# Reordering an attention stage around its gate: a later exponential, four weight quarters, another order for the last chunk

## The chip, the cores and the metric

The kernel runs on one core of a Trainium2 chip. Its time is the device time of one execution in microseconds. TensorE (PE) multiplies matrices, VectorE (DVE), ScalarE (ACT) and GpSimd (POOL) do the rest, and SyncE (SP) issues most of the DMAs; GpSimd issues gathers, scatters and the DMAs that add to what lies in SBUF. Each engine takes its instructions in order. TensorE has a granted clock of 2.4 GHz or half of it.

## The reference

Three layers follow each other. In short:

```
attention (B=2, H=8, S=768, D=48), a linear recurrence per head:
    y[t] = r[t] . (state + (u * k[t]) v[t]^T)
    state = w * state + k[t] v[t]^T
x = y as 1536 tokens of 384
gate: logits = x @ w_gate (8 experts); e = argmax; p = softmax(logits)[e]
    a token has the next free place of its expert; over capacity it is dropped (row 0)
experts: out = p * (relu(x @ w1[e]) @ w2[e]),  w1: 384 x 1024, w2: 1024 x 384
last layer: h = out @ w_in; s = h * softmax(h); layer norm with g_ln; out = ln @ w_out
```

All is float32. The kernel gets near float32 out of single-pass matmuls by splitting an operand in two parts: hi, the rounded value, and lo, the remainder; a product is hi*hi + hi*lo + lo*hi.

## The kernel before, in words

**Attention (to about 85 us).** The 1536 tokens are 12 chunks of 128, six to a batch element. A loop over m = 0..11 does chunk m, and prepares later ones. In the order of the code, a step does: the decay of the state (`decay`, ScalarE), the scores of chunk m+1 (TensorE) and their mask (`mask_scores`, L295, VectorE), the products of chunk m+2 with the decay tables (`prelude`, GpSimd), and then `attend(m)`: `values`, `carry` (the state's part) and `attended` (A*v, L324) add up in PSUM, and ScalarE evicts them (L330). `between` inside `attend` is `ranks(m - 1)`: three small matmuls that count, for each token, how many earlier ones chose the same expert. In steps 1 and 11 they stand behind A*v, in the others ahead of it. `gate2(m - 1)` makes the slot of each token of the chunk before from its rank (L426, L433, L438, L441, L444) and scales the tokens by their gate (L448); `scatter` writes the token numbers to their slots in DRAM, `store` the tokens. `state(m)` updates the state (L362, L366, L371). `tokens(m)` turns chunk m back to tokens and multiplies by w_gate (L382). `gate1(m)` takes the argmax: sum the logits (L391, "lg" in what follows), smallest of the negated ones (L394), candidates (L396), maximum (L402), one-hot row (L404); between the candidates and the maximum the code issues the exponential with its sum on ScalarE (L399). Logits, candidates and rank product share one PSUM bank, and the program guards such a bank against two engines at once.

Beside this the loop loads raw expert weights in halves of 128 x 1536 (`load_half`, four buffers, the table `halves` says in which step) and splits quarters of 128 x 768 (`split_q`): hi on ScalarE (L115), lo on VectorE (L121). With `by_dma`, ScalarE writes -raw, rounded as hi is, into lo (L124), and a DMA issued by GpSimd adds the raw weights to it from DRAM (L119). With `defer=True` the low part waits in `pend` and is issued in the next step, interleaved with `gate2`. Six quarters are split in steps 4 to 9, the sixth by DMA.

**Last chunks.** Expert 0's tokens of chunks 0 to 7 are gathered from DRAM (L93); those of chunks 8 to 11 are placed by matmuls with a one-hot matrix (`place`, L539), with hi and lo of the tokens (`part`, `other`). After chunk 11 the code does gate1, part of gate2, ranks and the placing, then splits the result (L668, L670), and the experts begin. Slots of chunk 11 are scattered, and then expert 1's rows can be gathered: ids (L85) from DRAM, then the rows (L93).

**Experts (to about 221 us).** 32 steps g, four to an expert, each with 18 matmuls of `mm1(g)` (L793) and, two steps later, 18 of `mm2(g)` (L779 to L781). `xe_split` transposes the rows of the next expert (L772) and splits them. Each step also splits a quarter of w1 and of w2 for later steps; of w2, every fourth low part is made by DMA. Buffers: four each of hi and lo, for w1 and w2. Pieces of the last layer's weights are loaded and decoded between.

**Last layer (to the end).** Matmuls, softmax, norm and a scatter of the result per 128 rows.

Of the kernel before, what the change touches and what calls it, by code (L numbers as in the profile page):

```python
# [35 lines left out]
def rwkv_moe_solu_kernel(  # L36
# [95 lines left out]
    def attention(actx):  # L132
# [167 lines left out]
        def attend(m, between):  # L300
# [3 lines left out]
            late = m in (1, NM - 1)  # L304

# [30 lines left out]
            if not late:  # L336
                between()
# [4 lines left out]
            if late:  # L342
                between()
# [44 lines left out]
        def gate1(m):  # L388
            xp = xps[m]
            lg, eqd = banks[m][0:2]  # L390
            V.tensor_reduce(lg, xp[:, :, 2 * D:XW].rearrange("p a e -> p e a"), AX.X, ALU.add, negate=True)  # L391
            yield
            nmx = sm.tile([128, 1], F32, tag="nmx", name=f"nmx{m}")
            V.tensor_reduce(nmx, lg, AX.X, ALU.min)  # L394
            yield
            V.scalar_tensor_tensor(eqd, lg, nmx, desc, ALU.is_le, ALU.mult)  # L396
            ex = sm.tile([128, NE], F32, tag="ex", name=f"ex{m}")
            gs = sm.tile([128, 1], F32, tag="gs", name=f"gs{m}")
            S.activation(ex, lg, AF.Exp, bias=nmx, scale=-1.0, accum_out=gs)  # L399
            yield  # L400
            m2 = sm.tile([128, 1], F32, tag="m2", name=f"m2{m}")
            V.tensor_reduce(m2, eqd, AX.X, ALU.max)  # L402
            yield
            V.tensor_scalar(oh_all[:, m, :], eqd, m2, None, ALU.is_equal)  # L404
            gst[m] = (m2, gs)
            yield
# [11 lines left out]
        def gate2(m):  # L418
            m2, gs = gst.pop(m)
            oh, rk1 = oh_all[:, m, :], rank_all[:, m:m + 1]  # L420
            t1 = sm.tile([128, 1], F32, tag="t1", name=f"t1{m}")
            if m < NM - 2:
                S.activation(t1, m2, AF.Copy, scale=float(-RS), bias=float(NE * RS))
            else:
# [10 lines left out]
            if m == NM - 1:  # L435
                yield
            junk = sm.tile([128, NE], F32, tag="junk", name=f"junk{m}")
            V.scalar_tensor_tensor(junk, rps.pop(m), 1.0, oh, ALU.mult, ALU.mult, accum_out=rk1)  # L438
            yield
            t2 = sm.tile([128, 1], F32, tag="t2", name=f"t2{m}")  # L440
# [5 lines left out]
            yield  # L446
            xg = a2.tile([128, HP, 2 * D], F32, tag="xg", name=f"xg{m}", bufs=LAST + 1)
            S.activation(xg, raw[m][0], AF.Copy, scale=gate)  # L448
            xgs[m] = xg.rearrange("p a d -> p (a d)")
            yield  # L450
# [112 lines left out]
        halves = {2: (1, 0), 4: (2, 0), 5: (1, 1), 6: (2, 1), 7: (1, 2), 8: (1, 3), 10: (2, 2)}  # L563
        pend = []
        for m in range(NM):
            if m != NM - 2:
                decay(m)
            if m == NM - 2:
                pend.pop()()
# [10 lines left out]
            if m == NM - 1:  # L580
                steps = gate2(m - 1)
# [4 lines left out]
                onehots[m - 2] = place(m - 2)  # L586
            elif m:
                together(gate2(m - 1), single(*pend))
                pend.clear()
            if m == NM - LAST + 1:  # L590
                xe0 = load_xe(0, 0, 2, 1 + (NM - LAST) * C, ld.tile([128, 3, DM], F32, tag="kvr", name="xe0"))
            if m + 2 < NM:
                products = prelude2(m + 2)
                next(products)
            if m:
                scatter(m - 1)
            if m < NM - 2:
                state(m)
            tokens(m)
# [6 lines left out]
            if m == NM - 3:  # L606
                decay(m + 1)
# [14 lines left out]
            if 4 <= m < NM - 2:  # L622
                i = m - 4
                pend.append(split_q(1 + (i // 2) % 2, 2 * (i // 4) + i % 2, m == NM - 3, defer=True))
# [22 lines left out]
        next(steps), next(steps)  # L647
        ranks(m)
        onehots[m - 1] = place(m - 1)
        next(steps)  # L650
        onehots[m] = place(m)
        next(steps), next(steps)
        his[m] = part(m)
        together(steps)
        for i in (m - 1, m):
            los[i] = other(i, his[i])
        store(m)
# [22 lines left out]
    def experts_and_solu():  # L680
# [212 lines left out]
        for q in (2, 3):  # L893
            split_q(2, q, False)
        load_piece(0)
        load_piece(1)
        load_half(1, 4)
        for g in range(NQ + 2):
# [15 lines left out]
            if g + 4 < NQ:  # L914
                split_q(1, g + 4, False)
            if 2 <= g < NQ - 2:
                split_q(2, g + 2, g % 4 == 0)
# [6 lines left out]
            if g % 2 and g < NQ:  # L924
                j = (g + 1) // 2
                if 4 < j + 3 < NQ // 2:
# [251 lines left out]
```

## Time and profile before

| | |
|---|---|
| time, median of 3 runs | 344.92 us (343.88 to 345.94) |
| profiled execution | 343.56 us, its span 341.8 us |
| busy | PE 320.6, DVE 244.2, ACT 191.4, POOL 145.7 us |
| granted TensorE clock | 0.982 of 2.4 GHz, mean over the span |
| DMA | 56.61 MB, mean 166 GB/s |

The span counts from the first instruction to the last. Busy times are sums over stages that have different limits, so they have to be read stage by stage. In rows of the trace, times are microseconds from the span's start; L with a number is a line of the kernel; what stands in brackets is how long the engine was idle ahead of the instruction, and which engine's work ended that.

### The profile page before, as it was taken

The numbers are of one execution on the slowest core, as the hardware profiler recorded it, in microseconds if no ns is written. First come the engines' busy times: TensorE is split into PE (matmuls) and PEld (weight loads), VectorE is DVE, ScalarE is ACT, GpSimd is POOL, SyncE is SP. The second block draws the span as 40 slices with busy tenths as digits, with TensorE's granted clock in tenths as the row PEclk, the third lists the DMA queues.
The fourth block names the chain that finished last, engine by engine and source line by source line (L and its number), as shares of the span: only waits on it lengthen the run. The fifth ranks groups of instructions, "written<-read, shape, count | busy, mean of one in ns | idle before, by whom it ended". The sixth has DMA issues, their size and how long they took to land. (4 is left out here: it accounts for less than half of the span.)

```text
span 341.8 us, 7242 instructions
## 1 busy us (share of the span) xinstructions
PE 320.6 (94%) x2656; PEld 297.6 (87%) x2656; DVE 244.2 (71%) x572; ACT 191.4 (56%) x409; POOL 145.7 (43%) x198
## 2 busy tenths in 40 slices
PE   7999977988999999999999999898999999999990
PEld 3788866877999999999999999886999999999990
DVE  8988898976688999998999897365674444444410
ACT  1455646674666787878786956323654444433420
POOL 7977778855314422313241506503333233333321
PEclk9999999998799999999999999999999999999996
DMA  7988899528667989889798933000000000000010
GB/s 226 384 312 284 294 348 324 204 75 202 200 213 271 243 309 306 269 289 296 254 287 279 279 125 52 10 2 1 2 23 23 25 23 23 25 23 25 24 46 23
DMA packets 20394, 56.61 MB, mean 166 GB/s; under 512 B 6594, under 2 KB 8900, under 8 KB 20356
## 3 DMA queue, kind: packets, MB, share of 16 engines
q1 hardware_dynamic: 16772, 47.67, 40.9%
q0 software_dynamic: 3584, 8.46, 10.5%
q8 instruction: 21, 0.34, 0.4%
q14 instruction: 17, 0.14, 0.1%
HBM read 50.96 MB, written 5.16 MB: 164 GB/s over the span
## 5 line engine op out<-in xcount | busy, mean ns | idle before, releaser
L115 ACT ACTIVATE whi<-raw 128x768 fp32r<-128x768 f32 x64 | 52.2, 845 | 7.2 <-PE yps L780 3.5
L121 DVE TENSOR_TENSOR wlo<-raw,whi 128x768 fp32r<-128x768 f32 x56 | 52.1, 962 | 1.1 <-ACT whi L115 0.7
L780 PE MATMUL yps<-hl,whi 128*128 128x224 f32 x192 | 52.8, 275 | 0.0
L779 PE MATMUL yps<-hh,whi 128*128 128x224 f32 x192 | 52.7, 275 | 0.0
L781 PE MATMUL yps<-hh,wlo 128*128 128x224 f32 x192 | 52.4, 273 | 0.0
L1011 POOL TENSOR_SCALAR e<-e,nmu 128x1024 f32<-128x1024 f32 x12 | 13.5, 1122 | 65.8 <-DVE nmu L1010 65.8
L988 DVE TENSOR_REDUCE nm<-h 128x1 f32<-128x1024 f32 (+1 forms) x13 | 14.8, 1140 | 31.2 <-PE h L977 31.2
L780 PEld LDWEIGHTS yps<-hl,whi 128*128 128x128 f32 x192 | 36.9, 192 | 0.0
L781 PEld LDWEIGHTS yps<-hh,wlo 128*128 128x128 f32 x192 | 36.9, 192 | 0.0
L779 PEld LDWEIGHTS yps<-hh,whi 128*128 128x128 f32 x192 | 36.9, 192 | 0.0
L119 POOL DMA_DIRECT2D wlo<-in_w x8 | 7.9, 988 | 64.6 <-ACT wlo L124 55.3
L1045 PE MATMUL o<-w_hi,shi 128*128 128x384 f32 x96 | 33.1, 345 | 0.0
L1046 PE MATMUL o<-w_lo,shi 128*128 128x384 f32 x96 | 32.2, 335 | 0.0
L1047 PE MATMUL o<-w_hi,slo 128*128 128x384 f32 x96 | 32.2, 335 | 0.0
L93 POOL DMA_INDIRECT xe<-xs,ids x16 | 18.4, 1148 | 25.6 <-PE xt L772 15.1
L793 PE MATMUL hps<-xhi,whi 128*128 128x224 f32 x192 | 28.3, 285 | 0.4 <-ACT xhi L668 0.4
L793 PE MATMUL hps<-xlo,whi 128*128 128x224 f32 x192 | 27.3, 279 | 0.0
L793 PE MATMUL hps<-xhi,wlo 128*128 128x224 f32 x192 | 27.2, 279 | 0.0
L800 DVE SCALAR_TENSOR_TENSOR hl<-hps,hh 128x448 fp32r<-128x448 f32 x32 | 19.8, 620 | 10.0 <-ACT hh L799 8.3
L793 PEld LDWEIGHTS hps<-xhi,whi 128*128 128x128 f32 x192 | 25.2, 199 | 0.4 <-ACT xhi L668 0.4
L793 PEld LDWEIGHTS hps<-xhi,wlo 128*128 128x128 f32 x192 | 24.6, 196 | 0.0
L793 PEld LDWEIGHTS hps<-xlo,whi 128*128 128x128 f32 x192 | 24.6, 196 | 0.0
(182 smaller groups left out, 790.3 us busy)
## 6 DMA issues: line engine op xcount, KB each, us to landing
raw<-in_w SPq DMA_DIRECT2D x32, 768.0 KB, 6.7
kvr<-in_kvr SPq DMA_DIRECT2D x12, 576.0 KB, 6.0
rkT<-in_rkT SPq DMA_DIRECT2D x12, 512.0 KB, 7.2
wlo<-in_w POOLq DMA_DIRECT2D x8, 384.0 KB, 6.7
w<-in_w_in SPq DMA_DIRECT2D x8, 384.0 KB, 5.1
w<-in_w_out SPq DMA_DIRECT2D x8, 384.0 KB, 5.6
xs<-xg SPq DMA_DIRECT2D x12, 192.0 KB, 4.0
xe<-xs,ids POOLq DMA_INDIRECT x16, 6.4
```

Source lines behind the costliest of these rows:

```text
L93: nc.gpsimd.indirect_dma_start(out=t[0:n, b, :], out_offset=None, in_=xs[0:rows, :], in_offset=bass.IndirectOffsetOnAxis(ap=ids[0:n, e, c: ...
L115: S.activation(hi, raw, AF.Copy)
L121: V.tensor_tensor(lo, raw, hi.bitcast(F32), ALU.subtract)
L779: T.matmul(ps, w[0][ws], x[0][xsl], start=first, stop=False, skip_group_check=True)
L780: T.matmul(ps, w[0][ws], x[1][xsl], start=False, stop=False, skip_group_check=True)
L781: T.matmul(ps, w[1][ws], x[0][xsl], start=False, stop=last, skip_group_check=True)
L793: T.matmul(ps[:, f], w1s[g][i][:, kk, wf], x[j][:, kk], start=not (i or j or f or kk), stop=j == 1 and kk == KD - 1, skip_group_check=True,)
L800: V.scalar_tensor_tensor(hl, ps, 0.0, hh.bitcast(F32), ALU.max, ALU.subtract)
L988: V.tensor_reduce(nms[j], ps, AX.X, ALU.max, negate=True)
L1045: T.matmul(ps, hi[:, f % 4], wo[0][:, f], start=f == 0, stop=False)
L1046: T.matmul(ps, hi[:, f % 4], wo[1][:, f], start=False, stop=False)
L1047: T.matmul(ps, lo[:, f % 4], wo[0][:, f], start=False, stop=f == KF - 1)
```

## The change

- `attend`: the ranks of the chunk before stand behind A*v in all steps.
- `gate1`: the exponential is issued behind the one-hot row.
- The loop: `gate2` is no longer interleaved with the deferred low part; that now comes behind `scatter` and `state`, ahead of the products of chunk m+2. `decay(m + 1)` stands at the end of the state's work, no longer at the start of the next step. The row placement of chunk 9 goes ahead of `gate2(10)`.
- Weights: four quarters are split in the attention loop, in steps 4 to 7, none by DMA; five halves are loaded there, not seven. Two quarters and two halves move to the front of the experts. In the expert loop each quarter is split one step nearer to its use: w1 three steps ahead, w2 three steps ahead of its matmuls; the DMA-made low parts are those of the same seven w2 quarters, issued in steps g with g % 4 == 1, and halves are loaded in even steps.
- Last chunk: ranks right after `gate1`, then gate and rank product, hi of the tokens and their stored copy (`whole`), both placements, both low parts, and only then the slot.

```diff
--- before.py
+++ after.py
@@ -301,8 +301,6 @@
             c = m % CB
             A, tvn = As.pop(m)[0], chunks[m][1][:, 1]
             ys = a2.tile([128, HP, C], F32, tag="ys", name=f"ys{m}")
-            late = m in (1, NM - 1)
-
             def carry(yp, j, p):
                 if c:
                     T.matmul(
@@ -333,14 +331,11 @@
                 values(p)
             for p in range(HP):
                 carry(yps[p // 2], p % 2, p)
-            if not late:
-                between()
             for p in range(HP):
                 attended(p)
                 if p % 2:
                     evict(p // 2)
-            if late:
-                between()
+            between()
             yss[m] = ys
             rts.pop(m, None)
 
@@ -394,14 +389,14 @@
             V.tensor_reduce(nmx, lg, AX.X, ALU.min)
             yield
             V.scalar_tensor_tensor(eqd, lg, nmx, desc, ALU.is_le, ALU.mult)
+            yield
+            m2 = sm.tile([128, 1], F32, tag="m2", name=f"m2{m}")
+            V.tensor_reduce(m2, eqd, AX.X, ALU.max)
+            yield
+            V.tensor_scalar(oh_all[:, m, :], eqd, m2, None, ALU.is_equal)
             ex = sm.tile([128, NE], F32, tag="ex", name=f"ex{m}")
             gs = sm.tile([128, 1], F32, tag="gs", name=f"gs{m}")
             S.activation(ex, lg, AF.Exp, bias=nmx, scale=-1.0, accum_out=gs)
-            yield
-            m2 = sm.tile([128, 1], F32, tag="m2", name=f"m2{m}")
-            V.tensor_reduce(m2, eqd, AX.X, ALU.max)
-            yield
-            V.tensor_scalar(oh_all[:, m, :], eqd, m2, None, ALU.is_equal)
             gst[m] = (m2, gs)
             yield
 
@@ -419,9 +414,10 @@
             m2, gs = gst.pop(m)
             oh, rk1 = oh_all[:, m, :], rank_all[:, m:m + 1]
             t1 = sm.tile([128, 1], F32, tag="t1", name=f"t1{m}")
+            last = m == NM - 1
             if m < NM - 2:
                 S.activation(t1, m2, AF.Copy, scale=float(-RS), bias=float(NE * RS))
-            else:
+            elif not last:
                 V.tensor_scalar(t1, m2, float(-RS), float(NE * RS), ALU.mult, ALU.add)
             V.tensor_scalar(gs, gs, 1e-9, None, ALU.add)
             if m + 2 < NM:
@@ -432,11 +428,13 @@
             gate = sm.tile([128, 1], F32, tag="gate", name=f"gate{m}")
             V.reciprocal(gate, gs)
             raw[m] = xps.pop(m)[:, :, 0:2 * D], gate
-            if m == NM - 1:
+            if last:
                 yield
             junk = sm.tile([128, NE], F32, tag="junk", name=f"junk{m}")
             V.scalar_tensor_tensor(junk, rps.pop(m), 1.0, oh, ALU.mult, ALU.mult, accum_out=rk1)
             yield
+            if last:
+                V.tensor_scalar(t1, m2, float(-RS), float(NE * RS), ALU.mult, ALU.add)
             t2 = sm.tile([128, 1], F32, tag="t2", name=f"t2{m}")
             V.tensor_scalar(t2, rk1, float(cap), float(2 * NX), ALU.is_ge, ALU.mult)
             yield
@@ -444,10 +442,14 @@
             V.tensor_scalar(slot, rk1, t1, t2, ALU.add, ALU.add)
             slots[m] = slot
             yield
+            if not last:
+                whole(m)
+            yield
+
+        def whole(m):
             xg = a2.tile([128, HP, 2 * D], F32, tag="xg", name=f"xg{m}", bufs=LAST + 1)
-            S.activation(xg, raw[m][0], AF.Copy, scale=gate)
+            S.activation(xg, raw[m][0], AF.Copy, scale=raw[m][1])
             xgs[m] = xg.rearrange("p a d -> p (a d)")
-            yield
 
         def together(*steps):
             steps = list(steps)
@@ -560,13 +562,10 @@
                 V.scalar_tensor_tensor(three(xl), xp, gate, three(xh).bitcast(F32), ALU.mult, ALU.subtract)
             return xl
 
-        halves = {2: (1, 0), 4: (2, 0), 5: (1, 1), 6: (2, 1), 7: (1, 2), 8: (1, 3), 10: (2, 2)}
+        halves = {2: (1, 0), 4: (1, 1), 5: (2, 0), 6: (2, 1), 7: (1, 2)}
+        first = {4: (1, 0), 5: (1, 1), 6: (1, 2), 7: (2, 0)}
         pend = []
         for m in range(NM):
-            if m != NM - 2:
-                decay(m)
-            if m == NM - 2:
-                pend.pop()()
             if m:
                 if m + 1 < NM:
                     scores(m + 1)
@@ -578,24 +577,27 @@
             if m == NM - 2:
                 state(m)
             if m == NM - 1:
+                onehots[m - 2] = place(m - 2)
                 steps = gate2(m - 1)
                 for _ in range(4):
                     next(steps)
                 his[m - 1] = part(m - 1)
                 together(steps)
-                onehots[m - 2] = place(m - 2)
             elif m:
-                together(gate2(m - 1), single(*pend))
-                pend.clear()
+                together(gate2(m - 1))
             if m == NM - LAST + 1:
                 xe0 = load_xe(0, 0, 2, 1 + (NM - LAST) * C, ld.tile([128, 3, DM], F32, tag="kvr", name="xe0"))
-            if m + 2 < NM:
-                products = prelude2(m + 2)
-                next(products)
             if m:
                 scatter(m - 1)
             if m < NM - 2:
                 state(m)
+            while pend:
+                pend.pop()()
+            if m + 2 < NM:
+                products = prelude2(m + 2)
+                next(products)
+            if m < NM - 2:
+                decay(m + 1)
             tokens(m)
             if m + 2 < NM:
                 together(gate1(m), products)
@@ -603,8 +605,6 @@
                 prelude3(m + 2)
             elif m + 1 < NM:
                 together(gate1(m))
-            if m == NM - 3:
-                decay(m + 1)
             if NM - LAST < m < NM - 1:
                 if m < NM - 2:
                     onehots[m - 1] = place(m - 1)
@@ -619,9 +619,8 @@
                 load_half(*halves[m])
             if m == NM - LAST:
                 load_ids(0, 1)
-            if 4 <= m < NM - 2:
-                i = m - 4
-                pend.append(split_q(1 + (i // 2) % 2, 2 * (i // 4) + i % 2, m == NM - 3, defer=True))
+            if m in first:
+                pend.append(split_q(*first[m], False, defer=True))
 
 
         m = NM - 1
@@ -644,16 +643,15 @@
         add(m - 3, los)
         together(gate1(m))
         steps = gate2(m)
-        next(steps), next(steps)
         ranks(m)
-        onehots[m - 1] = place(m - 1)
-        next(steps)
-        onehots[m] = place(m)
-        next(steps), next(steps)
+        next(steps), next(steps), next(steps)
         his[m] = part(m)
-        together(steps)
+        whole(m)
+        for i in (m - 1, m):
+            onehots[i] = place(i)
         for i in (m - 1, m):
             los[i] = other(i, his[i])
+        together(steps)
         store(m)
         scatter(m)
         load_ids(1, 2)
@@ -890,11 +888,12 @@
         xraw = load_xe(1, 0, 2)
         dec = None
         most = []
-        for q in (2, 3):
-            split_q(2, q, False)
+        split_q(1, 3, False)
+        split_q(2, 1, False)
         load_piece(0)
         load_piece(1)
-        load_half(1, 4)
+        load_half(1, 3)
+        load_half(2, 2)
         for g in range(NQ + 2):
             e, q = divmod(g, 4)
             if q == 0 and (e + 1) * W < YW:
@@ -911,19 +910,21 @@
                 mm2(g - 2)
             if tokens and not e:
                 xe_split(e + 1, xraw)
-            if g + 4 < NQ:
-                split_q(1, g + 4, False)
-            if 2 <= g < NQ - 2:
-                split_q(2, g + 2, g % 4 == 0)
+            if g and g + 3 < NQ:
+                split_q(1, g + 3, False)
+            if g == 0:
+                split_q(2, 2, False)
+            if 2 <= g < NQ - 1:
+                split_q(2, g + 1, g > 4 and g % 4 == 1)
             if tokens and e:
                 xe_split(e + 1, xraw)
             if tokens and e + 2 < NE:
                 xraw = load_xe(e + 2, 0, 2)
             if g % 2 and g // 2 + 2 < 2 * NP:
                 load_piece(g // 2 + 2)
-            if g % 2 and g < NQ:
-                j = (g + 1) // 2
-                if 4 < j + 3 < NQ // 2:
+            if g % 2 == 0 and g:
+                j = g // 2
+                if j + 3 < NQ // 2:
                     load_half(1, j + 3)
                 if j + 2 < NQ // 2:
                     load_half(2, j + 2)
```

## Rows read from the trace of the kernel before

**Rows 1.** Stretches: us, busy by engine (PE, PEld, DVE, ACT, POOL), clock, DMA share, GB/s
```profile
19.14:41.09 21.95, 21.04 (x278) 18.66 (x276) 19.00 (x70) 13.47 (x45) 16.35 (x19) 1.00 0.85 280
41.09:65.86 24.77, 20.48 (x264) 17.71 (x263) 22.13 (x71) 13.56 (x43) 20.89 (x21) 1.00 0.89 314
...
90.50:221.00 130.50, 130.48 (x1173) 130.30 (x1172) 114.36 (x212) 95.30 (x170) 43.95 (x60) 1.00 0.76 236
```

**Rows 2.** Waits, 20 to 90 us: total, times, longest
```profile
DVE m L402 <- ACT ex L399: 5.5, 11, 0.7
```

**Rows 3.** DVE in order of time, 46 to 51 us (start, us, what)
```profile
46.25 0.17 DVE L402 TENSOR_REDUCE m<-xp 128x1 f32<-128x8 f32 x1 [0.48 <-ACT ex L399]
...
48.25 1.18 DVE L121 TENSOR_TENSOR wlo<-raw,whi 128x768 fp32r<-128x768 f32 x1
...
50.53 0.19 DVE L391 TENSOR_REDUCE xp<-xp 128x8 f32<-128x32 f32 x1
```

**Rows 4.** DVE in order of time, 72 to 84 us
```profile
72.41 1.22 DVE L295 TENSOR_TENSOR A<-sp,mask 128x1024 f32<-128x1024 f32 x1
...
75.59 0.19 DVE L391 TENSOR_REDUCE xp<-xp 128x8 f32<-128x32 f32 x1
...
78.56 1.26 DVE L539 SCALAR_TENSOR_TENSOR P<-iota_w,rank_all,oh_all 128x224 fp32r<-128x224 f32 x1
79.75 0.18 DVE L391 TENSOR_REDUCE xp<-xp 128x8 f32<-128x32 f32 x1
...
81.09 0.23 DVE L404 TENSOR_SCALAR oh_all<-xp,m 128x8 bf16<-128x8 f32 x1
...
81.55 0.43 DVE L539 SCALAR_TENSOR_TENSOR P<-iota_w,rank_all,oh_all 128x224 fp32r<-128x224 f32 x1
...
82.66 0.27 DVE L444 TENSOR_SCALAR slot<-rank_all,t,t 128x1 int32<-128x1 f32 x1
82.85 1.13 DVE L560 SCALAR_TENSOR_TENSOR xl<-xp,gate,xh 128x384 fp32r<-128x384 f32 x2
```

**Rows 5.** PE in order of time, 74 to 88 us
```profile
74.30 1.14 PE L382 MATMUL xp<-sel,ys 112*128 112x104 f32 x8 [0.88 <-ACT ys L330]
...
81.37 0.18 PE L410 MATMUL xp<-oh_all,mask_b 128*128 128x8 bf16 x1 [1.15 <-DVE oh_all L404]
...
85.51 1.70 PE L793 MATMUL hps<-xhi,whi 128*128 128x224 f32 x6 [0.36 <-ACT xhi L668]
```

**Rows 6.** ACT in order of time, 47 us and 73 us
```profile
47.64 0.76 ACT L330 ACTIVATE ys<-yp 112x256 f32<-112x256 f32 x2 [0.69 <-PE yp L324]
...
73.16 0.83 ACT L124 ACTIVATE wlo<-raw 128x768 fp32r<-128x768 f32 x1
```

**Rows 7.** POOL in order of time, 88 us
```profile
88.72 1.05 POOL L93 DMA_INDIRECT xe<-xs,ids  x1 [4.54 <-DMA ids<-idx]
```

**Rows 8.** Stretches behind the attention stage, columns as in rows 1
```profile
83.00:84.00 1.00, 0.82 (x5) 0.64 (x5) 0.98 (x2) 0.16 (x1) 0.79 (x1) 0.81 0.59 195
...
85.50:90.50 5.00, 4.99 (x23) 4.99 (x24) 2.84 (x9) 2.57 (x6) 1.47 (x2) 0.51 0.46 122
```

**Rows 9.** PE in order of time, 100 us
```profile
100.04 0.74 PE L772 MATMUL xt<-ident,xe 128*128 128x128 f32 x6
```

**Rows 10.** DMA issues by tile, 60 to 80 us, then 85 to 99: us to landing last
```profile
xe<-xs,ids POOLq DMA_INDIRECT x2, 3.3
...
xe<-xs,ids POOLq DMA_INDIRECT x2, 7.9
```

**Rows 11.** Line L119, 100 to 215 us
```profile
DMA to landing us min/median/max: 5.2/6.6/7.4
```

**Rows 12.** PE in order of time, 208 to 217 us
```profile
208.76 0.83 PE L793 MATMUL hps<-xhi,whi 128*128 128x224 f32 x6
...
216.80 0.27 PE L779 MATMUL yps<-hh,whi 128*128 128x224 f32 x1
```

**Rows 13.** ACT in order of time, 208 us
```profile
208.35 1.03 ACT L822 ACTIVATE yThi<-yps 128x448 f32 x2
```

More of the change, by code (lines that the diff above doesn't have):

```diff
@@ L396, in gate1 @@
             V.scalar_tensor_tensor(eqd, lg, nmx, desc, ALU.is_le, ALU.mult)
-            ex = sm.tile([128, NE], F32, tag="ex", name=f"ex{m}")
-            gs = sm.tile([128, 1], F32, tag="gs", name=f"gs{m}")
-            S.activation(ex, lg, AF.Exp, bias=nmx, scale=-1.0, accum_out=gs)
             yield
@@ L404, in gate1 @@
             V.tensor_scalar(oh_all[:, m, :], eqd, m2, None, ALU.is_equal)
+            ex = sm.tile([128, NE], F32, tag="ex", name=f"ex{m}")
+            gs = sm.tile([128, 1], F32, tag="gs", name=f"gs{m}")
+            S.activation(ex, lg, AF.Exp, bias=nmx, scale=-1.0, accum_out=gs)
             gst[m] = (m2, gs)
```

## The prediction

> **What bounds the kernel now.** I read the table of stretches first. Between 90.50 and 221 us the expert stage keeps TensorE busy for 130.48 of 130.50 us [rows 1]; nothing that VectorE, ScalarE or the queues lose there counts until it makes TensorE wait. The attention stage ahead of it is another case. Its steps can be timed by VectorE's mask of the scores (L295), one per chunk, at 19.14 (chunk 2's), 41.09 (chunk 6's), 65.86 (chunk 10's) and 72.41 (chunk 11's) [rows 1, 4]. The first four steps take 21.95 us, 5.49 each, with VectorE busy 4.75, TensorE 5.26, GpSimd 4.09, ScalarE 3.37 of it; the next four take 24.77, 6.19 each, with 5.53, 5.12, 5.22 and 3.39 [rows 1]. So VectorE leads by its in-order queue, and TensorE is close behind in the early steps. What VectorE waits for is one thing: the list of waits has the row maximum L402 behind the exponential L399 11 times, 5.5 us, 0.48 in the step shown [rows 2, 3]. The end of the stage is a chain over one chunk: lg of chunk 10 at 75.59, lg of chunk 11 at 79.75, its one-hot row from 81.09 (done 81.32), first expert matmul at 85.51 [rows 4, 5]. And there TensorE's granted clock falls: 0.81 of full from 83 to 84 and 0.51 from 85.5 to 90.5 (1.2 GHz instead of 2.4), after two stalls of 0.88 and 1.15 us [rows 5, 8].
>
> **Part by part.** All sums are against the profiled execution's own 343.56 us (a span of 341.8 and 1.76 around it, left as they are), which is 1.36 under the median of 344.92.
>
> *Exponential behind the one-hot row.* VectorE's maximum no longer waits 0.48 us. The exponential now starts after the one-hot row and ends some 0.5 later; its reader is the next step's L426, behind the 1.22 us mask, so in the loop it is hidden. It is late only for ScalarE's eviction L330 of the next chunk, queued behind it (and behind an 0.83 copy where a quarter is split). From the row maximum (46.25) to the next lg (50.53) VectorE had 4.28 us of work with a low part of 1.18, so 3.1 without [rows 3]. On the other path are 0.4 to the end of the one-hot row (0.17 and 0.23), 0.5 for the exponential, 0.8 for the eviction and 1.1 for the token matmuls [rows 3 to 6]: 2.8, and 3.6 with the copy, which only steps with a low part have. So no new wait, with 0.3 to 0.7 to spare. Gain: 0.48 in step 0. In the four steps to 41.09 VectorE would need 5.01, TensorE 5.26; it has some 0.6 in hand at the start. I take 5.1, so 1.55 (bounds 0.9 and 1.9). In the next four VectorE still leads: 4 x 0.48 = 1.9. To 65.86 that is 3.9.
>
> *Ranks behind A\*v.* TensorE no longer holds A\*v until the one-hot row of the chunk before is there; that keeps A\*v out of the 2.8 above, and I count nothing beside. The ranks wait for the exponential too, since both use one bank; their reader L438 comes over 1.2 us later.
>
> *Four quarters, not six; low parts behind the slots.* Step 9 (65.86 to 72.41, 6.55 us) loses one L121 (0.95 to 1.18, [rows 3]; 0.9 in its issue time) and its 0.48: 5.17, but TensorE's 5.2 binds: 1.35. In step 10, TensorE's token matmuls waited 0.88 for an eviction that stood behind two ScalarE copies of 0.83 for the sixth quarter; these and GpSimd's accumulating DMA go: 0.85 [rows 5, 6]. Behind the slot, a low part delays the same lg as before and lets the scatter go 0.9 earlier. Two quarters move to the experts' front, 1.9 us of VectorE in a stage where it is busy 114.36 of 130.50 [rows 1]. By the end of step 2 both orders have split six quarters there, so nothing is denser.
>
> The Trainium skill ("SBUF — State Buffer", Who interferes with whom) speaks against new neighbours: a VectorE instruction with two SBUF inputs and a GpSimd one that reads SBUF exclude each other. One row placement took 1.26 us, another 0.43 [rows 4], which agrees. By the rule a moved low part could be lengthened again; a rival below prices that.
>
> *Decay behind the state.* Four small ScalarE instructions move behind the state's copies; ScalarE is busy 3.4 of 5.5, so 0. If that cover went, they would cost their 1.0 per step.
>
> *Row placement of chunk 9 earlier.* It cost 1.26 us just ahead of the last lg (78.56 to 79.75), and now fills a wait for the ranks. TensorE's own chain allows 0 to 0.8; I take 0.4.
>
> *Last chunk.* Its 0.48 goes: 0.48. From the one-hot row's end (T) to the first expert matmul it was 85.51 - 81.32 = 4.19. Now L426 waits for the exponential (T+0.5), the rank product is read at T+0.8 (was T+0.58), the two placements follow to T+1.85 and the two low parts (1.13, [rows 4]) to T+2.95 (was T+2.66). The last three placing matmuls then end near T+3.45, the split and first matmul follow 0.44 later as they do now: T+3.9. Gain 0.3 (bounds -0.5 and 0.8).
>
> Sum to the first expert matmul: 0.48 + 1.55 + 1.9 + 1.35 + 0.85 + 0.4 + 0.48 + 0.3 = 7.3.
>
> *The clock.* With both stalls gone, TensorE has placing matmuls to do until the experts begin, and I expect the clock to stay at 2.4 GHz. At half clock, 23 matmuls took 5.00 us (0.217 each) against 0.111 (1173 in 130.50): 23 x 0.106 = 2.4 [rows 1, 8]. Bounds 0 and 2.4; I take 2.4, as 0.88 + 1.15 is most of the idle time ahead of the fall. The Trainium skill ("TensorE: Matmul & The Clock Gate", Why this matters for your kernels) says the same, that idle gaps between bursts bring the half rate; by it the 2.4 is earned in full unless the next item makes a new gap.
>
> *The slot of the last chunk, now last.* Its scatter leaves after both low parts. It was ready at T+1.61 (82.66 + 0.27) and is now at about T+3.45. On GpSimd's and SyncE's queues the chain scatter, ids, gather follows: the first gather went out at 88.72, 5.8 after the slot [rows 7], so now T+9.25, which is 5.3 after the first expert matmul (was 3.2), the second 1.4 later. Landing takes 3.3 on light queues and 7.9 here [rows 10]: 10 to 14.6 after that matmul. SyncE also has one more half of weights to load at this point. TensorE came to the transposes of these rows at 100.04, 14.5 after [rows 9], at full clock 12.1. So it waits 0 to 2.5; near the row of this place, 1.6.
>
> *Splits a step later in the experts.* A step is 130.5/32 = 4.1 us and a quarter is still used 2.5 to 3 steps after its split, so 0, and ScalarE no longer waits for TensorE to free the buffer. The seven quarters whose low part a DMA adds have least room. For the last, the matmuls of quarter 27 end at 208.76; eviction to 209.4 [rows 13], two copies of 0.83 and 0.3 for the issue give 211.35, and the matmuls that read it come at 216.80 [rows 12]: 5.5 us for a landing of 5.2 / 6.6 / 7.4 (shortest, median, longest, [rows 11]). At the other six there is one more group of 18 matmuls (2.0) and 0.7 of transposes, less a copy: about 7.4. So none to a few tenths each; I take 0.4 for all (bounds 0 and 5).
>
> Total: 7.3 + 2.4 - 1.6 - 0.4 = 7.7 off 343.56 = 335.9, and with the 1.36 to the median **337.2 us**.
>
> **Rivals.**
> 1. *Something takes the wait's place in the steps.* Evictions behind the exponential hold the tokens, or the four moved low parts meet GpSimd's reads (1.26 - 0.43 = 0.83 each, 3.3). For: GpSimd is busy 5.22 of 6.19. Against: that leaves it a microsecond of each step, and ScalarE nearly three. The 3.9 of the steps falls to about 0.6: 340.5.
> 2. *The late rows of expert 1 take the clock with them.* A landing of 7.9 plus 2 for the added half gives a wait of 4.5 and then 2.4 at half clock: 337.2 + (4.5 - 1.6) + 2.4 = 342.5. For: that half; against: queues are emptier just before.
> 3. *The loads bound the stage.* The DMA share is 0.85 and 0.89 in the two stretches [rows 1]. If chunks can't come faster, only the tail's 1 to 2 us stays, and late rows eat it: 344.
> 4. *Slower: the accumulating DMA lands late in each expert.* Place: the seven quarters above. Price: what a landing takes beyond 7.4. From 1.3 us each (8.7 from issue), 7 x 1.3 = 9.1 eats the gain and more; at 2 each, 337.2 + 14 = 351. For: at the longest landing no margin is left. Against: only one of the seven quarters has less than 7.4 us.
>
> **How the numbers follow.** Forecast 0.58 (own range 335 to 339.5), rival 1 0.17, rival 2 0.11, rival 3 0.07, rival 4 0.05, better than 335 0.02. The range is 334.5 to 342.2: it takes in the forecast, rival 1 and part of 2. About 0.5% (1.7 us) is what can be told from no change: faster is below 343.2 and holds forecast, rivals 1 and 2 and a little of 3, 0.87; within 0.08; slower 0.05.
>
> **What would show it.** Right: L402 no longer waits; masks some 5.1 apart in steps 1 to 4 and 5.7 in 5 to 8; first expert matmul near 78.2; clock at 1.00 there; a short wait at L772 for the gather. Wrong: lg waiting for L382, L121 above 1.2, a granted clock near 0.5 behind the first expert matmul, or TensorE idle ahead of L781 once in every expert.

## The result, and the profile after

The changed kernel takes 340.53 us (median of 4 runs, 339.11 to 340.68), beside 344.84 for the kernel before on the same chip (343.88 to 345.94): ratio 0.9865, 95% interval 0.9825 to 0.9904. 337.2 was predicted. The profiled execution took 340.68, its span 338.9 (341.8 before).

Stretches of the changed kernel: us, busy by engine (PE, PEld, DVE, ACT, POOL), clock, DMA share, GB/s. The first two answer to [rows 1] (chunks 2 to 6, 6 to 10), the third is the expert stage, the last lies behind it.
```profile
18.84:39.56 20.72, 20.72 (x276) 18.39 (x272) 19.35 (x69) 12.86 (x46) 17.34 (x19) 1.00 0.87 286
39.56:63.07 23.51, 21.70 (x279) 18.77 (x278) 22.18 (x72) 14.22 (x48) 20.36 (x21) 1.00 0.84 327
79.84:215.84 136.00, 134.19 (x1194) 133.13 (x1194) 118.01 (x221) 98.33 (x176) 46.94 (x62) 1.00 0.77 243
218.88:222.40 3.52, 3.52 (x8) 2.83 (x9) 1.71 (x3) 0.61 (x1) 0.00 (x0) 0.52 0.02 2
```
Two things are to be seen. The attention steps are shorter, and the first four are now TensorE's: it is busy all 20.72 us. And the half clock at the start of the experts [rows 8] is gone, but there is one at a new place, 218.88 to 222.40.

TensorE in order of time: the tokens of chunks 10 and 11, the ranks of chunk 11, the first expert matmul (answers to [rows 5]), and the end of the experts:
```profile
69.80 1.14 PE L377 MATMUL xp<-sel,ys 112*128 112x104 f32 x8
...
73.70 1.14 PE L377 MATMUL xp<-sel,ys 112*128 112x104 f32 x8 [0.27 <-ACT ys L328]
...
76.51 0.17 PE L405 MATMUL xp<-oh_all,mask_b 128*128 128x8 bf16 x1 [0.39 <-ACT ex L399]
...
79.84 0.37 PE L791 MATMUL hps<-xhi,whi 128*128 128x224 f32 x1 [0.38 <-issue]
...
215.57 0.27 PE L779 MATMUL yps<-hh,wlo 128*128 128x224 f32 x1
218.88 1.64 PE L978 MATMUL h<-w_hi,yThi 128*128 128x512 f32 x3 [3.04 <-ACTq L1122]
```
The stall of 0.88 ahead of chunk 10's tokens is gone (chunk 11's now wait 0.27), that of 1.15 is 0.39, and the first expert matmul comes 5.67 earlier. But at the passage from the experts to the last layer TensorE stands for 3.04 us, "ACTq L1122" being ScalarE's queue at the branch around the overflow code; before it stood 1.13 there.

What TensorE waited for inside the expert stage (total, times, longest), and the landing of expert 1's gather (L93, answers to [rows 10]):
```profile
PE xt L770 <- DMA xe<-xs,ids: 1.5, 3, 0.7
...
PE yps L779 <- DMA wlo<-in_w: 0.3, 1, 0.3
```
```profile
DMA to landing us min/median/max: 8.0/8.0/8.0
```
VectorE in step 8, and from the slot of step 10 to the end (answers to [rows 3, 4]); L394, the maximum that waited for the exponential, waits no more, L386 is lg:
```profile
59.02 0.27 DVE L442 TENSOR_SCALAR slot<-rank_all,t,t 128x1 int32<-128x1 f32 x1 [0.45 <-ACT xg L451]
...
62.26 0.17 DVE L394 TENSOR_REDUCE m<-xp 128x1 f32<-128x8 f32 x1
...
71.20 0.27 DVE L442 TENSOR_SCALAR slot<-rank_all,t,t 128x1 int32<-128x1 f32 x1 [0.52 <-ACT t L419]
71.39 0.19 DVE L386 TENSOR_REDUCE xp<-xp 128x8 f32<-128x32 f32 x1
...
74.88 0.20 DVE L386 TENSOR_REDUCE xp<-xp 128x8 f32<-128x32 f32 x1 [0.73 <-PE xp L377]
...
76.88 0.81 DVE L541 SCALAR_TENSOR_TENSOR P<-iota_w,rank_all,oh_all 128x224 fp32r<-128x224 f32 x2
77.60 1.14 DVE L562 SCALAR_TENSOR_TENSOR xl<-xp,gate,xh 128x384 fp32r<-128x384 f32 x2
```

### The profile page after: what moved, and what is told of

Same layout as the page of the kernel before. It is cut to its first block, busy times and chain, and to the rows that moved or that the text cites. A ratio compares the mean times of both kernels' runs of the same rounds, so it can differ in the third digit from the quotient of the medians.

```text
span 338.9 us, 7222 instructions
## 1 busy us (share of the span) xinstructions
PE 321.2 (95%) x2656; PEld 296.6 (88%) x2656; DVE 244.2 (72%) x573; ACT 190.2 (56%) x408; POOL 145.0 (43%) x197
## 5 line engine op out<-in xcount | busy, mean ns | idle before, releaser
L115 ACT ACTIVATE whi<-raw 128x768 fp32r<-128x768 f32 x64 | 50.8, 840 | 0.0
L119 POOL DMA_DIRECT2D wlo<-in_w x7 | 6.9, 984 | 69.7 <-ACT wlo L124 69.7
L791 PE MATMUL hps<-xhi,whi 128*128 128x224 f32 x192 | 27.5, 278 | 0.4 <-issue 0.4
L791 PEld LDWEIGHTS hps<-xhi,whi 128*128 128x128 f32 x192 | 24.2, 192 | 0.6 <-issue 0.5
L93 POOL DMA_INDIRECT xe<-xs,ids x16 | 17.8, 1115 | 15.4 <-DMA ids<-idx 11.3
L978 PE MATMUL h<-w_hi,yThi 128*128 128x512 f32 x72 | 21.3, 405 | 3.2 <-ACTq L1122 3.0
```

Source lines behind the costliest of these rows:

```text
L93: nc.gpsimd.indirect_dma_start(out=t[0:n, b, :], out_offset=None, in_=xs[0:rows, :], in_offset=bass.IndirectOffsetOnAxis(ap=ids[0:n, e, c: ...
L115: S.activation(hi, raw, AF.Copy)
L791: T.matmul(ps[:, f], w1s[g][i][:, kk, wf], x[j][:, kk], start=not (i or j or f or kk), stop=j == 1 and kk == KD - 1, skip_group_check=True,)
L978: T.matmul(ps[j], col(x, kk, ts_), wi[w][:, kk, fs], start=not (i or kk), stop=i == 2 and kk == KD - 1,)
```

## The experiments

All twelve in one table. Ratios are to the kernel before on the same chip, with 95% intervals; the rest is one profile each, so differences of a few tenths in it say little. *Place*: ScalarE's instructions ahead of the branch L1122, counted in the trace; *ScalarE*: from its branch to its next waiting instruction; *idle*: TensorE from the last expert matmul to the last layer; *rest*: from there to the end.

```
kernel        ratio [interval]         place ScalarE  1st expert  experts  idle  rest
before                                  465   0.47     85.51      135.47   1.13  119.72
changed       0.9865 [0.9825, 0.9904]   450   2.30     79.84      136.00   3.04  120.05
after_again   0.9876 [0.9839, 0.9912]   450   1.93     79.60      135.60   2.12  118.40
pad15         0.9852 [0.9820, 0.9884]   434   0.47     79.61      135.23   1.29  118.39
exp_back      1.0005 [0.9981, 1.0029]   450   1.92     83.68      135.09   2.10  120.01
ranks_ahead   0.9904 [0.9874, 0.9933]   450   1.96     79.70      135.12   2.14  120.03
weights_old   0.9835 [0.9804, 0.9865]   465   0.46     82.53      133.66   1.26  118.49
early_slot    0.9870 [0.9834, 0.9906]   450   2.11     80.10      135.25   2.28  119.72
loads_first   0.9987 [0.9959, 1.0014]   450   1.90     79.60      138.84   2.08  118.41
last_old      0.9870 [0.9836, 0.9904]   450   1.92     79.81      135.13   2.10  118.42
pad_back      0.9804 [0.9774, 0.9835]   465   0.47     79.45      134.83   1.29  118.37
wo_short      0.9863 [0.9827, 0.9899]   450   1.92     80.96      133.37   2.10  120.12
lo_pad        0.9800 [0.9768, 0.9831]   434   0.47     80.04      135.61   1.29  118.35
rests_ahead   0.9892 [0.9854, 0.9930]   450   2.08     80.95      134.97   2.26  118.42
```

### The stall behind the branch
**pad15**: tiny copies in the experts, to shift ScalarE's code.
```diff
...
+            if 2 <= g < 17:
+                S.activation(pad, tot[:, 0:1], AF.Copy)
             if g == 0:
                 load_ids(2, NE)
```


> The changed kernel with 15 copies of one column (128x1) more on ScalarE, one in each expert step from 2 to 16, where it has room. Theory 1 (where ScalarE's code is cut into fetched pages): behind the branch at the end of the experts ScalarE stood still for 2.30 us in the changed kernel and 0.47 in the one before, and its stream was 15 instructions shorter up to that branch (450 against 465); with 15 more the gap goes back to about 0.5 us, TensorE's idle there from 3.0 to about 1.1, its clock stays at 1.00, and the time falls by about 2.3, to 338.2. Theory 2 (the gap comes from something else at this passage, as the branch's value or DMA work): the gap stays at 2.3 and the time at 340.5 to 340.8.

The stall went, but the count didn't go as I thought: the copies took over waits that had been instructions of their own (107 ahead of the branch became 76), and the place became 434, not 465. So the theory had been met by another place than the one it named, and two kernels followed in which only the number of copies was chosen for the place.

**after_again**: the changed kernel unedited.

> The changed kernel once more, as the reference for the three beside it. Theory 1 (the stall behind the branch hangs on where ScalarE's code is cut, since a kernel with the same number of ScalarE instructions showed it again and one with another number did not): ScalarE stands 1.9 to 2.3 us behind the branch again, ratio near 0.9865. Theory 2 (the stall was chance): gap about 0.5, ratio near 0.977.

**pad_back**: as pad15, in other steps and number.
```diff
...
+            for _ in range({14: 8, 15: 8, 16: 7, 17: 7}.get(g, 0)):
+                S.activation(pad, tot[:, 0:1], AF.Copy)
```


> The changed kernel with 30 copies of one column on ScalarE in expert steps 14 to 17, so many that with the waits they take over its branch stands at place 465 of its stream again, where it stands in the kernel before (450 in the changed one; the 15 of the earlier run took over waits and put it at 434). Theory 1 (the stall hangs on the place of the code): ScalarE goes on about 0.5 us behind the branch, TensorE is idle 1.1 to 1.3 us there at full clock, time 0.8 to 2.5 under the changed kernel's, ratio 0.979 to 0.985. Theory 2 (the copies of the earlier run helped in another way, by shortening the stream or by the waits they took over): stall of 1.9 again, ratio 0.987.

**wo_short**: the weights of before (weights_old, below) with copies.
```diff
...
+            for _ in range(2 <= g < 20):
+                S.activation(pad, tot[:, 0:1], AF.Copy)
```


> The changed kernel with the weights as before, which had no stall (branch at place 465), with 18 copies of one column on ScalarE in expert steps 2 to 19, one each, which take over waits, so that the branch stands at 450. Theory 1 (place of the code): the stall of 1.9 to 2.3 us comes up in a kernel that had none, TensorE idle 2.1 or more there, ratio 0.9835 + 0.003 to 0.007, 0.9865 to 0.990. Theory 2: gap 0.5, ratio 0.9835.

ScalarE at the branch, pad_back (the times at the end of a line are its first and last start), then what TensorE waits for there in pad_back and in wo_short:
```profile
L1125 ACTq EVENT_SEMAPHORE  x2: 17/17/17, 214.9 to 214.9; - x2
...
L1125 ACTq COMPARE_BRANCH  x1: 68/68/68, 214.4 to 214.4; - x1
```
```profile
PE h L981 <- DVEq L1125: 1.3, 1, 1.3
```
```profile
PE h L978 <- ACTq L1122: 2.1, 1, 2.1
```
And the same two rows of the changed kernel:
```profile
L1122 ACTq EVENT_SEMAPHORE  x2: 17/17/17, 218.8 to 218.9; - x2
...
L1122 ACTq COMPARE_BRANCH  x1: 68/68/68, 216.5 to 216.5; - x1
```
All nine profiles with the branch at 450 stall (1.90 to 2.30 us), whatever else differs; the five at 434 or 465 don't (0.46 or 0.47). pad_back has the stream of the changed kernel plus copies and is cured, wo_short is a cured kernel made to stall. That the place decides, of the three tried, is shown. In time, the four changed kernels without the stall have medians of 336.4 to 337.0 us; after_again, ranks_ahead, early_slot, last_old, wo_short and rests_ahead, which stall, have 337.9 to 339.0. (The changed kernel's first four runs had 340.53, where the kernel before was slower too; exp_back and loads_first lose elsewhere.)

Why is partly seen. In all nine a code fetch of 8 KB starts 0.27 to 0.78 us behind ScalarE's branch, and ScalarE goes on 1.13 to 1.32 us after the end of that fetch (changed kernel: branch 216.51, fetch 217.29 to 217.60, on at 218.81). In the other five ScalarE has gone on before any fetch starts (1.06 to 1.32 behind the branch). The Trainium skill ("Runtime: NRT & Kernel Launch", Instruction fetch mechanics) says that a taken branch to code outside the fetched window holds the engine until it is fetched; the trace agrees, with 1.9 to 2.3 us. ScalarE's prefetch hint, an instruction some 10 us ahead of the branch, doesn't tell the two groups apart: a fetch follows it within 0.4 us in the kernel before and in weights_old, but none within 4 us in pad15, pad_back and lo_pad, which don't stall either. Which places are bad, no run derives.

In five of the nine half clock follows the stall and the rest takes 119.7 to 120.1, not 118.4. The code alone doesn't set which: the changed kernel has it, the same kernel run again (after_again) hasn't.

### The parts of the change, undone one by one
**exp_back**: the exponential ahead of the maximum.
```diff
             V.scalar_tensor_tensor(eqd, lg, nmx, desc, ALU.is_le, ALU.mult)
+            S.activation(ex, lg, AF.Exp, bias=nmx, scale=-1.0, accum_out=gs)
             yield
...
```


> The changed kernel with the exponential back ahead of the row maximum of the candidates, all else as changed. Theory 1 (the prediction's sum): the maximum waits again some 0.48 us in every step, and the first expert matmul comes 0.48 + 1.55 + 1.9 + 0.48 = 4.4 later, at about 84.2; time about 344. Theory 2 (something else binds the steps now, TensorE's tokens or the slots of the scatter): it comes less than 2 us later, and the time is under 342.3.

Theory 1, nearly to size: 4.08 later than after_again (4.4 expected). VectorE's waits from 39.6 to 63.1 us, exp_back:
```profile
DVE m L397 <- ACT ex L394: 1.9, 4, 0.5
```
Without this one edit the time is where it was: ratio 1.0005. The other parts still bring the first expert matmul 1.83 earlier (83.68, 85.51 before); the stall behind the experts, which they bring too, takes 0.97 of it, and half clock follows it.

**rests_ahead**: the low parts among the gate's steps.
```diff
-                together(gate2(m - 1))
+                together(gate2(m - 1), single(*pend))
+                pend.clear()
...
-            while pend:
-                pend.pop()()
```


> The changed kernel with the low parts of the four quarters among the steps of the gate again, ahead of slot and scatter, as before. Theory 1 (the prediction: nothing either way for the same lg): first expert matmul within 0.3 of 79.6, masks 5 to 9 as far apart as now (5.74, 5.63, 5.90, 6.23). Theory 2 (behind the slot a low part runs beside the scatter of GpSimd, and both are stretched, which took part of what the steps were to gain): ahead of it the steps are 0.2 to 0.4 shorter each, first expert matmul 0.6 to 1.5 earlier.

Both theories fail. The steps 5 to 8 take 25.04 us, not 23.51: the move is worth 1.35 at the first expert matmul (80.95, 79.60 in after_again). VectorE's low part, first in rests_ahead, then in the changed kernel:
```profile
52.57 1.64 DVE L121 TENSOR_TENSOR wlo<-raw,whi 128x768 fp32r<-128x768 f32 x1
```
```profile
53.24 0.95 DVE L121 TENSOR_TENSOR wlo<-raw,whi 128x768 fp32r<-128x768 f32 x1
```
GpSimd beside it in rests_ahead, then in the changed kernel:
```profile
52.22 1.17 POOL L253 TENSOR_TENSOR kt<-rkT,TB 128x512 f32<-128x512 f32 x1
53.35 0.91 POOL L425 TENSOR_TENSOR acc<-acc,oh_all 128x8 bf16<-128x8 bf16 x1
```
```profile
52.45 0.19 POOL L425 TENSOR_TENSOR acc<-acc,oh_all 128x8 bf16<-128x8 bf16 x1
53.33 1.73 POOL L472 DMA_INDIRECT idx<-row,slot  x1 [0.70 <-DVE Sc L361]
```
Ahead of the slot the low part runs against GpSimd's products and takes 1.39 to 1.64 in four steps (0.95 to 1.20 in the kernel before, where it ran at another time beside them); behind it, 0.95. There it stretches the scatter, from 1.07 to 1.47 in two steps and from 1.33 to 1.73 in two, and no engine's list of waits has that scatter. The rule of the Trainium skill that the prediction weighed ("SBUF — State Buffer", Who interferes with whom) agrees with these rows, but I had it speak against the new place, and it spoke against the old one.

**ranks_ahead**: the ranks ahead of A*v, but for chunks 1 and 11.
```diff
...
+            if not late:
+                between()
             for p in range(HP):
                 attended(p)
...
```


> The changed kernel with the ranks ahead of A*v again, but for chunks 1 and 11, as before the change. Theory 1 (the prediction counted nothing for this edit by itself, since the waits of the ranks fall into TensorE's spare time): first expert matmul within 0.5 us of 79.84, time 340 to 341. Theory 2 (the exponential, which now ends last, holds the ranks and behind them A*v, the eviction and the tokens): the ranks' 1.8 us of waits become waits of the whole chain, 0.3 to 0.4 per step over ten steps, so 3 to 4 us later, time about 343.5 to 344.5.

Theory 1: 79.70, 0.10 later; steps 5 to 8 take 23.60. This move is worth nothing that can be told by itself.

**weights_old**: six quarters, the splits in the experts a step earlier.
```diff
-        halves = {2: (1, 0), 4: (1, 1), 5: (2, 0), 6: (2, 1), 7: (1, 2)}
+        halves = {2: (1, 0), 4: (2, 0), 5: (1, 1), 6: (2, 1), 7: (1, 2), 8: (1, 3), 10: (2, 2)}
...
-            if g and g + 3 < NQ:
-                split_q(1, g + 3, False)
+            if g + 4 < NQ:
+                split_q(1, g + 4, False)
...
```


> The changed kernel with the weights as before: six quarters split in attention, the last of them with a DMA-made low part, and the experts' splits one step earlier; all else as changed. Theory 1 (the prediction's sum): steps 9 and 10 get back 1.35 + 0.85 = 2.2 us, the first expert matmul is at about 82, the clock may fall there (up to 2.4 more), time 342.7 to 345. Theory 2 (the later split costs in the experts what it saves ahead of them): the time stays within 1 us of 340.5, the experts being shorter by what the attention stage is longer.

Both are true, one for each stage. The stall of chunk 10's tokens is back (1.33 behind L328) and half clock with it in this run; in wo_short, the same code but for copies in the experts, the stall is back and half clock isn't. TensorE's stretches, weights_old, then wo_short:
```profile
70.00:72.00 2.00, 0.77 (x5) 0.77 (x6) 1.30 (x7) 1.99 (x6) 1.39 (x3) 0.91 0.35 98
72.00:74.00 2.00, 2.00 (x12) 2.00 (x12) 1.19 (x7) 0.74 (x3) 1.92 (x3) 0.50 0.44 145
```
```profile
70.00:72.00 2.00, 0.77 (x7) 0.78 (x7) 1.24 (x7) 1.99 (x6) 1.41 (x2) 1.00 0.34 98
72.00:74.00 2.00, 2.00 (x24) 1.87 (x24) 1.54 (x8) 1.00 (x6) 1.97 (x3) 1.00 0.44 148
```
So the first expert matmul is 1.36 later at full clock (80.96), 2.93 with the fall (82.53). But TensorE then waits for no DMA in the experts: 133.4 to 133.7 us, beside 134.8 to 136.0 in the kernels with four quarters (138.8 in loads_first). In time the edit can't be told from nothing: with the stall 0.9863 (wo_short) against 0.9876 (after_again); without it 0.9835 (weights_old) lies between 0.9852 (pad15) and 0.9804 (pad_back, whose branch is at the same place).

**last_old**: the last chunk in the order of before.
```diff
...
-        next(steps), next(steps), next(steps)
-        his[m] = part(m)
-        whole(m)
-        for i in (m - 1, m):
-            onehots[i] = place(i)
+        onehots[m - 1] = place(m - 1)
+        next(steps)
+        onehots[m] = place(m)
+        next(steps), next(steps)
+        his[m] = part(m)
...
```


> The changed kernel with the last chunk in the order of before (one placement ahead of the gate's steps, slot ahead of the low parts, chunk 9's placement behind the steps of chunk 10). Theory 1 (the prediction's sum): first expert matmul 0.4 + 0.3 later, near 80.5, the late rows' waits (1.3) gone, time about 0.6 lower. Theory 2 (the last chunk's order is worth more, 1 us or over, as the tail fell from 13.10 to 11.40): first expert matmul at 81 or later, time the same or higher.

The first expert matmul is 0.21 later (0.7 by theory 1), the waits for late rows fall from 1.2 in after_again to 0.2, and a DMA-made low part takes 0.5: nothing in all that can be told (0.9870 against 0.9876).

### The late rows of expert 1
**early_slot** and **loads_first**:
```diff
-        next(steps), next(steps), next(steps)
+        for _ in range(5):
+            next(steps)
```


> The changed kernel with the slot of the last chunk ahead of its two row placements, not behind the low parts. Theory 1 (the late slot makes the late rows of expert 1): the scatter leaves some 1.9 us earlier, the two waits of TensorE for these rows (0.57 + 0.74 us) go, the first expert matmul comes 0.3 to 0.5 later, the time falls by 0.8 to 1.0. Theory 2 (SyncE issues two halves and two pieces of weights right behind the addresses, and the rows land behind them wherever the slot stands): the loads move with the slot, landing still takes 8 us; counted from the first expert matmul everything is about 2.3 earlier, so the waits go too, but the gather's landing time tells: 8 by theory 2, under 6 by a theory of chance in the queues.


```diff
+        split_q(1, 3, False)
+        load_half(1, 3)
         store(m)
         scatter(m)
         load_ids(1, 2)
...
```


> The changed kernel with one quarter (w1, quarter 3) split and one half of weights (768 KB) requested ahead of the last chunk's store, scatter and addresses, where the DMA queues stand empty for some 4 us, and not behind the addresses. Theory 1 (the rows of expert 1 are late because weights requested together with them fill the queues): the gather lands in 5 to 6.5 us, not 8, TensorE's two waits (1.3 us) shrink to under 0.3, first expert matmul within 0.3 of before; time 1.0 to 1.3 lower than the changed kernel's. Theory 2 (landing does not depend on that half): landing 8 and waits stay, time the same.

Neither did what was meant. In early_slot the scatter left 1.71 earlier and landed no earlier. GpSimd's scatter and its landing (the last number), early_slot, then after_again:
```profile
77.51 0.97 POOL L472 DMA_INDIRECT idx<-row,slot  x1 [2.12 <-DVE slot L442]
...
idx<-row,slot POOLq DMA_INDIRECT x1, 4.3
```
```profile
79.22 0.97 POOL L472 DMA_INDIRECT idx<-row,slot  x1 [3.84 <-DVE slot L442]
...
idx<-row,slot POOLq DMA_INDIRECT x1, 2.5
```
The addresses (L85) so went out at 81.86 and 81.78. In both, a code fetch of 16 KB for TensorE lies there (79.54 to 80.79 and 78.73 to 80.28), and the last packets of scatter or store come only behind it; that it holds them is read from the packets and not tried by itself. The gather's landing stayed at 7.8, as theory 2 has it. In loads_first the half had to wait for its split and went out at 79.83, just behind the start of the scatter (79.22); the scatter then landed after 5.9 us, and SyncE's addresses waited for it. What SyncE waited for, the scatter's landing and the gather's:
```profile
SPq L106 <- DVE wlo L121: 4.8, 1, 4.8
SPq L85 <- DMA idx<-row,slot: 4.4, 1, 4.4
```
```profile
idx<-row,slot POOLq DMA_INDIRECT x1, 5.9
```
```profile
DMA to landing us min/median/max: 6.3/6.4/6.6
```
The landing did shrink, 8.0 to 6.4, with one half less beside it, though the kernel before also has one half there and 7.9 [rows 10]. The gather started 3.3 later (87.54), and the experts took 3.2 more; of TensorE's waits in them the late rows have only 0.7, a DMA-made low part 1.4 and ScalarE's `hh` 1.0.

### A version ahead of both
**lo_pad**: last_old with the copies of pad15.

> The changed kernel with the last chunk in the order of before, which landed the rows of expert 1 a microsecond earlier, and 15 copies of one column on ScalarE, which put its branch at 434. Theory 1 (both losses that the change made are met): waits for the late rows under 0.5 us, no stall, no half clock; span 79.8 + 133.7 + 0.9 + 1.3 + 118.4 = 334.1, time near 335.9, ratio 0.980 to 0.983, the lowest of all. Theory 2 (the rows' waits go back and forth with the queues from run to run, and nothing is gained by the order): ratio as that of the earlier kernel with 15 copies, 0.985.

0.9800, with pad_back's 0.9804 the lowest, below the changed kernel's 0.9865 and 0.9876. By medians pad15, pad_back and lo_pad are alike (337.00, 336.44, 336.67 us); pad15's 0.9852 is higher since the kernel before took 342.06 beside it and 343.83 beside the two others. What all three lack is the stall. TensorE's wait for the rows was 0.05 in its profile, but there the experts began at a low clock (0.62 from 80.04 to 83, 0.81 to 86) and took 135.61, so TensorE came to the rows later; the order of the last chunk can't be told apart by it.

## Why the prediction was right, and where its sizes were off

The measured 340.53 is 3.3 above the forecast of 337.2 and outside the forecast's own range of 335 to 339.5. That it falls on rival 1's 340.5 is luck: of the 4.8 us by which the gain fell short, 1.6 lay in the steps up to the first expert matmul, and the largest single loss, 1.91, at a place that no rival named. By the two profiles (us gained):
```
                                           predicted   measured
start, steps 1 to 4                        0.48+1.55   0.30+1.23
steps 5 to 8                               1.9         1.26
step 9                                     1.35        1.18
step 10, to chunk 10's lg                  0.85        0.23
to chunk 11's lg                           0.4         0.67
to the first expert matmul                 0.48+0.3    0.80
   sum to the first expert matmul          7.3         5.67
clock (135.47 - 133.66)                    2.4         1.81
late rows of expert 1                     -1.6        -1.46
DMA-made low parts                        -0.4        -0.34
other time in the experts                  0          -0.54
passage to the last layer (3.04 - 1.13)    0          -1.91
last layer (120.05 - 119.72)               0          -0.33
   total                                   7.7         2.90
```
Shown is the exponential's wait (its 4.4 measured as 4.08) and the price of the late rows. The clock's 1.81 rests on weights_old's experts, which run at full clock and wait for no DMA; that the stalls ahead bring the fall is likely, not shown. lo_pad fell to half clock at the start of the experts after waits of 0.41, 0.39, 0.18 and 0.37 that last_old had too (0.42, 0.39, 0.18, 0.38), without a fall. In 44 runs of the kernel before beside the experiments the mean clock lies between 0.977 and 0.996, median 0.986; in pad15, pad_back and lo_pad the medians are 0.993 to 0.996. So the gain is there on average, and one pair of profiles can show more or less of it.

**The step sum is mis-sized by 1.6.** In steps 1 to 4 I took 5.1 and it was 5.18: TensorE binds, and the mask of chunk 6 comes at 39.0 to 39.6 in all changed kernels but exp_back (41.32), while that of chunk 2 wanders from 17.96 to 19.06. In steps 5 to 8 two steps gave 0.54 and 0.56, one 0.23, and the last nothing, since there the slot waits 0.45: something took the wait's place, as rival 1 has it, in one step of four. What makes that wait stays open. The sum had 1.9 here for the exponential alone and nothing for the low parts behind the slots. Neither does anything there alone: the four steps take 24.77 before, 25.20 in exp_back (low parts moved, exponential not), 25.04 in rests_ahead (exponential moved, low parts not), and 23.51 with both. So the parts don't add up to the whole.

In step 10 the 0.85 was read from TensorE's stall. That went whole, but chunk 10's lg came only 0.23 sooner, since VectorE stood 0.52 at the slot just ahead of lg, for ScalarE's `t`. The kernel before had such a wait too, which the prediction didn't read:
```profile
75.41 0.27 DVE L444 TENSOR_SCALAR slot<-rank_all,t,t 128x1 int32<-128x1 f32 x1 [0.99 <-ACT t L423]
```
Chunk 11's lg then waits 0.73 for its tokens, one of the signs that the prediction gave for being wrong; it costs little there, as the step came out 0.67 shorter where 0.4 was forecast.

**The passage was not in the sum at all.** I left all that lies behind the experts as it was. It cost 1.91 of idle time and half clock behind it (120.05 against 118.4, 1.66); the kernel before had a stall of its own in the last layer that went in the changed kernel, so that the rest shows only 0.33. TensorE there, before:
```profile
PE h L977 <- DVE e L1006: 1.4, 1, 1.4
```
**The change's weights part was no gain that can be told.** I had 2.2 for it in the attention stage and -1.6 for late rows elsewhere, as two items; they are one trade, 1.36 at the first expert matmul for 1.2 to 2.6 in the experts. Rivals 2 to 4 did not come: no half clock with the late rows, TensorE and VectorE and not the loads bind the steps, and the DMA-made low parts cost 0.34 in one expert of seven.

## What to carry to other kernels

Cost an edit to the end of the kernel: work that is taken from a tight stage and put at the front of the next is paid there, if a transfer is needed there too. A change in the number of an engine's instructions can cost or give 1 to 2 us at a branch far behind it; compare two versions there before their ratio is put down to the edit, and when a version is a little worse for no reason, look for an engine that stands still behind a branch. Undo each part by itself: here one part carried most, together with one that was thought neutral and without which it gave nothing in four steps, and three gave nothing that could be told.

## What the hardware showed

- A branch that skips code: ScalarE went on after 0.47 us with the branch at two places of its stream, after 1.9 to 2.3 at a third, in fourteen profiles without exception; in the slow ones 1.13 to 1.32 us after the end of an 8 KB code fetch.
- Half clock (0.52 for 3.5 us) after an idle time of 2.1 to 3.0 us came in five of nine profiles; in the other four the clock stayed at 1.00 after 2.08 to 2.26, once in the same kernel. The idle time alone doesn't decide.
- A VectorE subtraction of 128x768 took 0.95 alone and up to 1.64 beside GpSimd's products, which in turn went with a GpSimd addition of 128x8 that took 0.91, not 0.19; moved, it stretched a scatter from 1.33 to 1.73.
- TensorE's code arrives in 16 KB transfers of 0.9 to 1.8 us; in early_slot, where one lay behind the start of a small scatter's packets, the scatter landed after 4.3 us, not 2.5 (not tried by itself).
